# Block attention and MLP on one core: the same instructions in a new order, from a planner with other landing times and a charge for switches

## The chip, the cores and the metric

The kernel runs on one core of a Trainium2 chip. A core has TensorE (PE, matmuls and weight loads), VectorE (DVE), ScalarE (ACT), GpSimd (POOL), and SyncE (SP), which here issues the transfers. The metric is the device time of one execution in microseconds. The times before are 612.1, 612.23 and 613.61, median 612.23.

## The reference

An attention in which each query sees a band of 16 positions to either side and one summary for every block of 32 keys, and behind it an MLP with a gated activation.

```python
k_sum = k.reshape(B, H, nb, block, D).max(axis=3)          # B, H, S, D = 4, 8, 768, 64; block 32
v_sum = v.reshape(B, H, nb, block, D).mean(axis=3)
scores_l = where(|i - j| < 16, scale * q @ k^T, -1e9)
scores_s = scale * q @ k_sum^T + log(32)
a = softmax(concat([scores_l, scores_s]))
x = a @ concat([v, v_sum])                                 # 3072 tokens x 512
h = x @ w_in                                               # 512 x 2048
g = h * erf(maximum(h, 0) + log1p(exp(-|h|)))
out = g @ w_out                                            # 2048 x 512
```

## The kernel before

The 3072 tokens are worked on in 6 chunks of 512. For each chunk there are four blocks of attention (a pair of heads each) and four groups of the hidden layer (512 of the 2048 columns each). An attention block is: scores on PE (mask, window keys and key summaries; small matmuls of 64 rows), maximum on DVE, exponentials on ACT, normalisation on DVE or ACT, transposes of the weights, and the product with the values (16 small matmuls, tile px). The result is split in a rounded high part and a low rest (tiles xh, xl), and the MLP's products are three matmuls each on such parts: the hidden layer `h` (mm1, 128x512), in the later chunks sums of half-size products (`ha`, `hb`), and the output `ops` (mm2).

The order on every engine is found by a planner when the program is built. The code calls each step in a natural order and hands it to a class `Plan` with a cost in us for each engine that can do it, what it reads and what it writes. `Plan.order` then goes through time: it takes the engine that is free first, looks at the steps that are ready, and picks the one with the lowest key: its place in the natural order on PE, a due time on the other engines, each plus a correction from the table `TUNE`. A step that two engines can do goes to the one that ends first. Nothing of the plan's times is in the program; what stays is the order on each engine, and between engines the waits for data and for buffers. Engines work off their own order without overtaking.

Two things in it matter here. The first transfers are declared by `first_dma`, with a time in us that each occupies the transfer queue in the plan, in place of a size: keys and queries of the first block row (`load_qk_first`, tiles kf and qf), the values of the first sequence in two halves (`load_v_first`, vt), the window values (`load_vw_first`, vwf) and the first weights (rw). The value sums of the first sequence are six matmuls on the halves of the values (`vsum_first`, tile vs), three for each half. From them come the rows that are copied into the window values of each of the four blocks; for the last three blocks ACT or a transfer can do this copy. And where the plan sees PE idle before the first output product, the program puts filler matmuls (`busy`, tile idle), one for each 0.31 us of planned idle time:

```python
        if o["on"] == "PE":
            filling = filling and "o3" not in o["w"]
            if filling:
                busy(int(max(0.0, o["start"] - last) / 0.31))
            last = o["end"]
```

Of the kernel before, what the change touches and what calls it, by code (L numbers as in the profile page):

```python
# [23 lines left out]
NP = H // 2  # L24
# [6 lines left out]
LW = 96  # L31
# [5 lines left out]
MQ = NP  # L37
# [8 lines left out]
TABLE = 1.29  # L46
TTR = 1.52
# [9 lines left out]
class Plan:  # L57
# [6 lines left out]
    def add(self, eng, fn, r=(), w=(), after=(), table=None, hold=0.0, land=0.0):  # L64


        n, deps = len(self.ops), set(after)
        for x in r:
            deps.update(self.last.get(x, ()))
        for x in w:  # L70
            deps.update(self.last.get(x, ()))
            deps.update(self.readers.get(x, ()))
        for x in w:
            self.last[x], self.readers[x] = (n,), []
        for x in r:
            self.readers.setdefault(x, []).append(n)
        deps.discard(n)
        self.ops.append(dict(n=n, eng=eng, fn=fn, r=r, w=w, deps=deps, table=table, hold=hold, land=land))
        return n
# [22 lines left out]
    def order(self, free, window, tune, table):  # L102

        self.due()
        ops = self.ops
        wait = [len(o["deps"]) for o in ops]
        ready = [0.0] * len(ops)
        cand = {e: set() for e in free}  # L110
        pe = [o["n"] for o in ops if "PE" in o["eng"]]
        seq = {n: i for i, n in enumerate(pe)}
        head = 0
        done = [False] * len(ops)
        out = []
        key, change = {}, {}
        for o in ops:
            n = o["n"]
            later, change[n], which, eng = tune.get(n, (0.0, PEN, 0, None))
            key[n] = later + (n if "PE" in o["eng"] else o["due"])  # L120
            if eng is not None:
                o["eng"] = {eng: o["eng"][eng]}
                o["two"] = True
            if o["table"]:
                o["pick"] = o["table"][which]

        def open_(n):
            for e in ops[n]["eng"]:
                cand[e].add(n)

        for o in ops:
            o["two"] = o.get("two", False) or len(o["eng"]) > 1
            if not wait[o["n"]]:
                open_(o["n"])
        while len(out) < len(ops):
            best = None
            while head < len(pe) and done[pe[head]]:
                head += 1
            for e, c in cand.items():
                if e == "PE":  # L140
                    c = [n for n in c if seq[n] - head <= window(seq[n])]
                if not c:
                    continue
                t = max(free[e], min(ready[n] for n in c))
                if best is None or t < best[0]:
                    best = t, e, c
            t, e, c = best
            c = [n for n in c if ready[n] <= t + 0.05]
            n = min(c, key=lambda n: (key[n] + (change[n] if e == "ACT" and ops[n]["table"] and table not in ops[n]["table"] else 0.0), n))
            o = ops[n]  # L150
            if len(o["eng"]) > 1:
                ends = {x: max(free[x], ready[n]) + d for x, d in o["eng"].items()}
                x = min(ends, key=ends.get)
                if x != e and ends[x] < ends[e]:
                    cand[e].discard(n)
                    cand[x].add(n)
                    continue
            start = max(t, ready[n])
            end = start + o["eng"][e]
            if o["table"] and e == "ACT" and table not in o["table"]:  # L160
                table = o["load"] = o["pick"]
                end += TABLE
            free[e] = end
            o.update(on=e, start=start, end=end)
            done[n] = True
            out.append(o)
            if e == "SP":
                end += o["land"]
            for x in o["eng"]:
                cand[x].discard(n)  # L170
            for s in o["succ"]:
                ready[s] = max(ready[s], end + (LAT[e] if e == "SP" or e not in ops[s]["eng"] or ops[s]["two"] else 0.12 if e != "PE" else 0.0) + (ops[s]["hold"] if e != "SP" else 0.0))
                wait[s] -= 1
                if not wait[s]:
                    open_(s)
        return out
# [9 lines left out]
def block_attention_mlp(ctx: ExitStack, tc: tile.TileContext, q_t, k_nat, k_win, v_tok, v_nat, v_win, w_in, w_out, out):  # L186
# [78 lines left out]
    def pe(us, fn, r=(), w=(), **kw):  # L265
        return P.add({"PE": us}, lambda e: fn(), r, w, **kw)
# [10 lines left out]
    def first_dma(us, fn, r=(), w=(), **kw):  # L277
        return P.add({"SP": us}, lambda e: fn(), r, w, hold=2.0, land=-1.0, **kw)
# [210 lines left out]
    def load_qk_first(p):  # L489
        st[p] = dict(qb=qfs[:, p], vw=vws[p // 2][:, p % 2])  # L490
        first_dma(0.97, lambda: nc.sync.dma_start(out=kfirst[p], in_=k_nat[0, p]), w=[f"kf{p}"])
        first_dma(0.66, lambda: nc.sync.dma_start(out=qfs[:, p], in_=q_t[0, p]), w=[f"qf{p}"])

    def load_v_first():
        for n in range(2):
            first_dma(2.0, lambda n=n: nc.sync.dma_start(out=vts[n], in_=v_tok[3 * n:3 * n + 3].rearrange("t s c -> s t c")), w=[f"vt{n}"])

    def load_vw_first(p):
        first_dma(1.3, lambda: nc.sync.dma_start(out=st[p]["vw"], in_=v_win[0, p]), w=[f"vwf{p}"])
# [54 lines left out]
    def scores(qd, banks=PA):  # L554

        s = st[qd]

        def mask():
            for n in banks:
                tiles[n] = ps(n, n)  # L560
            s["sc"] = [tiles[n] for n in banks]
            m0 = mask_at[qd // NP % 3]
            for sc in s["sc"] if qd < MQ else []:

                nc.tensor.matmul(sc[:, 0:NI * NK], lhsT=ident_h, rhs=mask_h[:, m0:m0 + NI], start=True, stop=False, skip_group_check=True)
                nc.tensor.matmul(sc[:, 0:NI * NK].rearrange("q (i c) -> q i c", i=NI)[:, :, LW:NK], lhsT=ones, rhs=cst.rearrange("o (i c) -> o i c", i=NI), start=False, stop=False, skip_group_check=True)

        def keys(parts):
            for j in range(NB):
                for a in range(2):  # L570
                    r, o = slice(64 * a, 64 * a + 64), slice(64 * (j % 2), 64 * (j % 2) + 64)
                    for n, rhs in parts(r, j):
                        n += j // 2 * NK
                        nc.tensor.matmul(s["sc"][a][o, n:n + rhs.shape[-1]], lhsT=s["qb"][r, 64 * j:64 * j + 64], rhs=rhs, start=qd >= MQ, stop=True, skip_group_check=True)  # L574

        def near(r, j):

            kn, k0 = kfirst[qd], 64 * j - 16
            return [(0, kn[r, k0:k0 + LW])] if j else [(0, kn[r, 0:16]), (16, kn[r, 0:LW - 16])]

        def both():
            mask()
            keys(lambda r, j: [(0, s["kw"][r, j])])
        if qd >= NP:
            pe(1.06 if qd >= MQ else 1.64, both, [f"qb{qd % 2}", f"kw{qd % 2}"] + (["mh"] if qd < MQ else []), banks)
        else:
            pe(0.58, mask, ["mh"], banks)
            pe(0.96, lambda: keys(near), [f"qf{qd}", f"kf{qd}"], banks)
            pe(0.5, lambda: keys(lambda r, j: [(LW, ksum[r, 0, qd])]), [f"qf{qd}", f"ksum0{qd}"], banks)
# [47 lines left out]
    def transp(qd):  # L637
# [14 lines left out]
        if qd < DT:  # L652
            pe(0.95, go, [pr], PA)
            act(1.1, cp, PA, ["pt"])
            return
# [23 lines left out]
    def av(qd, bank):  # L679
        s = st[qd]  # L680
        s["bank"] = bank

        def go():
            xo = s["xo"] = ps("px", bank)
            for j in range(NB):
                o = slice(64 * j, 64 * j + 64)
                for a in range(2):
                    r = slice(64 * a, 64 * a + 64)
                    if qd < DT:
                        b = 64 * (NI * a + j // 2)  # L690
                        nc.tensor.matmul(xo[r, o], lhsT=s["vw"][0:NK, j, r], rhs=s["pt"][0:NK, j % 2, b:b + 64], start=True, stop=True)  # L691
                    else:
                        z = 2 * (j % 2)
                        nc.tensor.matmul(xo[r, o].rearrange("d (a q) -> d a q", a=2), lhsT=s["vw"][0:NK, j, r], rhs=s["pt"][0:NK, z:z + 2, NI * a + j // 2], start=True, stop=True)  # L694
        pe(1.08, go, ["pt", "vw"] if qd >= NP else ["pt", f"vwf{qd}", f"vwg{qd}"], [bank])
# [550 lines left out]
```

## Time and profile before

| what | us |
|---|---|
| median of 3 runs | 612.23 |
| the profiled execution's own time | 612.39 |
| its span, first to last instruction | 610.2 |
| PE busy with matmuls | 599.5 |
| DVE busy | 460.5 |
| ACT busy | 407.9 |

The mean granted TensorE clock is 0.996 of full speed. The page shows 40 slices of the span; PE is at 9 tenths or more in all but the first and the last. A row of a timeline has the start, the time, the engine, the line and operation, what is written and read, the shape, and in brackets idle time before it with its releaser. A releaser "issue" means that the engine waited for nothing that the profile shows. Matmuls overlap, so the distance between two starts is what one costs PE, and its own time is longer. SPq is SyncE's queue; a row there is the issue of a transfer, which lands later.

### The profile page before, as it was taken

The page shows a single profiled execution, that of the slowest core. Times are in us where ns is not written, and L with a number is a line of the kernel's source. Part 1 is how long each engine was busy: PE and PEld are TensorE (multiplying, and loading weights), DVE is VectorE, ACT ScalarE, POOL GpSimd, SP SyncE. Part 2 cuts the span into 40 slices and gives each one's busy share as a digit, 9 for nine tenths or more (in the row PEclk, how much of TensorE's full clock was granted, in tenths as well). Part 3 has the DMA queues.
Part 4 walks back from the last instruction along what each step waited for, and adds up shares of the span by engine and source line. Part 5 has one row for each costly group of instructions (what it writes and reads, how often), then busy time and mean ns, then how long its engine had stood idle before and what let it go on. Part 6 is the DMA issues. An engine that isn't in the chain of part 4 may idle for free.

```text
span 610.2 us, 12059 instructions
## 1 busy us (share of the span) xinstructions
PE 599.5 (98%) x4714; PEld 498.1 (82%) x4714; DVE 460.5 (75%) x915; ACT 407.9 (67%) x815; POOL 3.8 (1%) x28
## 2 busy tenths in 40 slices
PE   6999999999999999999999999999999999999997
PEld 4576656777888889889799899898898898899886
DVE  5899999969999997877889758669658537546442
ACT  5779959979789774873776764746667546652340
POOL 2000000000000000000000000000000000000000
PEclk9899999999999999999999999999999999999999
DMA  8979766568699689999898989888777774665622
GB/s 325 412 313 362 296 207 208 206 236 311 252 333 361 239 295 331 348 382 325 319 379 294 370 301 340 284 302 261 287 272 284 265 248 151 245 238 193 220 70 69
DMA packets 47751, 169.85 MB, mean 278 GB/s; under 512 B 4432, under 2 KB 17488, under 8 KB 35152
## 3 DMA queue, kind: packets, MB, share of 16 engines
q1 hardware_dynamic: 47120, 168.58, 76.2%
q8 instruction: 37, 0.61, 0.4%
q10 hardware_dynamic: 576, 0.52, 0.3%
q14 instruction: 18, 0.15, 0.1%
HBM read 135.66 MB, written 31.46 MB: 274 GB/s over the span
## 4 chain that ended last, share of the span: by engine, by line
PE 94%; ACT 2%; DVE 1%; DMA 1%; issue 1%; SPq 0%; ACTq 0%
PE ops L952 39%; PE hb L838 15%; PE h L797 14%; PE ha L838 11%; PE ops L948 5%; PE pA L574 3%; PE px L694 3%; PE vs L508 1%; DMA qf<-q_t 1%; PE px L691 1%; ACT prf L615 0%; ACT ptr L651 0%; PE pA L646 0%; ACT w L281 0%; PE pB L574 0%
## 5 line engine op out<-in xcount | busy, mean ns | idle before, releaser
L952 PE MATMUL ops<-w,gh 128*128 128x512 f32 x704 | 228.2, 393 | 0.0
L952 PEld LDWEIGHTS ops<-w,gh 128*128 128x128 f32 x704 | 132.6, 188 | 28.6 <-issue 1.1
L952 PE MATMUL ops<-w,gl 128*128 128x512 f32 x352 | 137.5, 391 | 0.0
L1203 ACT ACT_TABLE_LOAD x91 | 116.8, 1283 | 1.6
L928 DVE TENSOR_TENSOR hc<-wt,hc 128x1024 f32<-128x1024 f32 x44 | 52.8, 1221 | 60.7 <-ACT wt L916 60.6
L797 PE MATMUL h<-xh,w 128*128 128x512 f32 x256 | 86.8, 402 | 0.0
L281 ACT COPY hc<-hb 128x256 f32<-128x256 f32 x56 | 20.8, 371 | 85.5 <-DVE hc L891 31.3
L952 PEld LDWEIGHTS ops<-w,gl 128*128 128x128 f32 x352 | 66.2, 188 | 12.4
L615 ACT ACTIVATE prx<-prx,stats 128x120 f32<-128x120 f32 x160 | 61.0, 382 | 0.8 <-DVE stats L602 0.6
L797 PEld LDWEIGHTS h<-xh,w 128*128 128x128 f32 x256 | 48.0, 188 | 12.5 <-issue 1.1
L838 PE MATMUL hb<-w,ws 128*128 128x256 f32 x384 | 56.4, 283 | 0.0
L935 DVE TENSOR_TENSOR gl<-hc,gh 128x1024 fp32r<-128x1024 f32 x44 | 53.5, 1217 | 0.4
L838 PEld LDWEIGHTS hb<-w,ws 128*128 128x128 f32 x384 | 50.6, 192 | 0.1
L797 PE MATMUL h<-xl,w 128*128 128x512 f32 x128 | 50.2, 392 | 0.2 <-DVE xl L710 0.2
L916 ACT ACTIVATE wt<-wt 128x1024 f32<-128x1024 f32 x48 | 49.6, 1057 | 0.4
L904 ACT ACTIVATE wt<-hc 128x1024 f32<-128x1024 f32 x32 | 32.6, 1053 | 14.1 <-DVE hc L281 13.9
L281 DVE CAST gh<-hc 128x1024 fp32r<-128x1024 f32 x40 | 27.5, 688 | 11.2 <-PE ops L952 10.7
L659 DVE STREAM_TRANSPOSE ot<-prx 128x1024 f32<-128x1024 f32 x16 | 32.9, 2056 | 0.3
L615 ACT ACTIVATION_READ_ACCUMULATOR prx<-prx,stats 128x1 f32 x160 | 29.9, 187 | 0.0
L948 PE MATMUL ops<-a32s,gw 128*128 128x512 f32 x64 | 29.1, 597 | 0.0
L797 PEld LDWEIGHTS h<-xl,w 128*128 128x128 f32 x128 | 24.1, 188 | 6.0 <-DVE xl L710 1.0
L838 PE MATMUL ha<-xh,ws 128*128 128x256 f32 x128 | 28.3, 284 | 0.0
(166 smaller groups left out, 998.1 us busy)
## 6 DMA issues: line engine op xcount, KB each, us to landing
w<-dr SPq DMA_DIRECT2D x36, 1024.0 KB, 7.5
ws<-ds SPq DMA_DIRECT2D x30, 1024.0 KB, 6.5
vw<-v_win SPq DMA_DIRECT2D x20, 512.0 KB, 4.8
kw<-k_win SPq DMA_DIRECT2D x20, 480.0 KB, 3.5
rw<-w_in SPq DMA_DIRECT2D x8, 1024.0 KB
rw<-w_out SPq DMA_DIRECT2D x8, 1024.0 KB, 6.5
dr<-w SPq DMA_DIRECT2D x8, 1024.0 KB, 5.4
dt<-ot SPq DMA_DIRECT2D x16, 512.0 KB, 3.5
```

Source lines behind the costliest of these rows:

```text
L281: e.copy(o, i) if e is nc.scalar else e.tensor_copy(o, i)
L615: nc.scalar.activation(s["pr"][:, j], s["pr"][:, j] if qd >= MQ else s["sc"][j // NI][:, i * NK:(i + 1) * NK], AF.Exp, scale=-1.0 if qd >= ...
L659: e.transpose(out=s["ot"].rearrange("p k j q -> p j k q"), in_=prx.rearrange("p j (q k) -> p j k q", k=4))
L797: nc.tensor.matmul(hs[k, f][:, 0:T], lhsT=w[m], rhs=xt[ch, cc][x], start=(cc == 0 and n == 0), stop=(cc == 3 and n == 2))
L838: nc.tensor.matmul(shape, lhsT=w[m], rhs=y[l], start=first and c == 0 and i == 0, stop=c == 1 and i == 2, skip_group_check=True)
L904: nc.scalar.activation(wt[k, n], hc[k, n], AF.Softplus)
L916: act(0.96, lambda n=n: nc.scalar.activation(wt[k, n], wt[k, n], AF.Erf, scale=-1.0 if k < SOFT else 1.0), [s], [s], table=("sig",), after ...
L928: e.tensor_tensor(hc[k, n], wt.pop((k, n)), hc[k, n], op=ALU.mult)
L935: e.tensor_tensor(gs[k, n][1], hc.pop((k, n)), f32(gs[k, n][0]), op=ALU.subtract)
L948: nc.tensor.matmul(os_[ch, t], lhsT=x[0][:, i % 2, t * 128:(t + 1) * 128], rhs=w32["o", g, i // 2][:, i % 2], start=first, stop=last)
L952: nc.tensor.matmul(os_[ch, t], lhsT=x[y][:, i % 2, t * 128:(t + 1) * 128], rhs=w[m], start=first and n == 0, stop=last and n == 2)
L1203: nc.scalar.preload_act_table_set(sets[o["load"]])
```

## The change

The planner gets other numbers, and the order of every engine is made anew. The instructions are the same but for filler matmuls (11 behind the first seven before, 11 after, at other places) and for steps that now go to another of the engines that can do them: some hundred copies between DVE and ACT, and two of the row copies of the value sums from ACT to transfers.

- The second keys occupy the queue for 2.7 us in the plan, not 0.97; the two halves of the values 2.1 and 2.25, not 2.0; the window values 1.35, not 1.3.
- Steps of small matmuls are marked `small`. In the plan PE pays `SWITCH` = 0.09 us where such a step follows one of large matmuls.
- The costs of the small steps themselves are new: scores 0.98 and 1.56 (1.06 and 1.64), transposes 0.61 (0.95), products with the values 1.085 (1.08).
- The table `TUNE` is another one (1099 entries, before 1103).

```diff
 TABLE = 1.29
+SWITCH = 0.09
 TTR = 1.52
...
-    def add(self, eng, fn, r=(), w=(), after=(), table=None, hold=0.0, land=0.0):
+    def add(self, eng, fn, r=(), w=(), after=(), table=None, hold=0.0, land=0.0, small=False):
...
-        head = 0
+        head, was = 0, False
...
                 end += TABLE
+            if e == "PE":
+                end += SWITCH * (o["small"] and not was)
+                was = o["small"]
             free[e] = end
...
-        first_dma(0.97, lambda: nc.sync.dma_start(out=kfirst[p], in_=k_nat[0, p]), w=[f"kf{p}"])
+        first_dma(2.7 if p == 1 else 0.97, lambda: nc.sync.dma_start(out=kfirst[p], in_=k_nat[0, p]), w=[f"kf{p}"])
...
-            first_dma(2.0, lambda n=n: nc.sync.dma_start(out=vts[n], in_=v_tok[3 * n:3 * n + 3].rearrange("t s c -> s t c")), w=[f"vt{n}"])
+            first_dma(2.1 + 0.15 * n, lambda n=n: nc.sync.dma_start(out=vts[n], in_=v_tok[3 * n:3 * n + 3].rearrange("t s c -> s t c")), w=[f"vt{n}"])
...
-        first_dma(1.3, lambda: nc.sync.dma_start(out=st[p]["vw"], in_=v_win[0, p]), w=[f"vwf{p}"])
+        first_dma(1.35, lambda: nc.sync.dma_start(out=st[p]["vw"], in_=v_win[0, p]), w=[f"vwf{p}"])
...
-            pe(1.06 if qd >= MQ else 1.64, both, [f"qb{qd % 2}", f"kw{qd % 2}"] + (["mh"] if qd < MQ else []), banks)
+            pe(0.98 if qd >= MQ else 1.56, both, [f"qb{qd % 2}", f"kw{qd % 2}"] + (["mh"] if qd < MQ else []), banks, small=True)
...
-            pe(0.95, go, [pr], PA)
+            pe(0.61, go, [pr], PA, small=True)
...
-        pe(1.08, go, ["pt", "vw"] if qd >= NP else ["pt", f"vwf{qd}", f"vwg{qd}"], [bank])
+        pe(1.085, go, ["pt", "vw"] if qd >= NP else ["pt", f"vwf{qd}", f"vwg{qd}"], [bank], small=True)
```

What this does to the order is shown at three places. The first is SyncE's queue from its first transfer on; kf and qf are keys and queries of the four first blocks, vt the two halves of the values, rw a weight, vwf window values. Before:

```order
L491 DMA kf<-k_nat 128x768
L492 DMA qf<-q_t 128x512
L491 DMA kf<-k_nat 128x768
L492 DMA qf<-q_t 128x512
L491 DMA kf<-k_nat 128x768 x2
L492 DMA qf<-q_t 128x512
L496 DMA vt<-v_tok 128x3x512 x2
L317 DMA rw<-w_in 128x2048
L499 DMA vwf<-v_win 128x1024
L492 DMA qf<-q_t 128x512
L499 DMA vwf<-v_win 128x1024
L317 DMA rw<-w_in 128x2048
```

After:

```order
L495 DMA kf<-k_nat 128x768
L496 DMA qf<-q_t 128x512
L495 DMA kf<-k_nat 128x768
L496 DMA qf<-q_t 128x512
L500 DMA vt<-v_tok 128x3x512
L495 DMA kf<-k_nat 128x768
L496 DMA qf<-q_t 128x512
L500 DMA vt<-v_tok 128x3x512
L321 DMA rw<-w_in 128x2048
L495 DMA kf<-k_nat 128x768
L496 DMA qf<-q_t 128x512
L503 DMA vwf<-v_win 128x1024 x2
```

The first half of the values moved from eighth to fifth place, ahead of the third keys and queries; the fourth keys moved behind the second half and the first weight.

The second place is PE about the value sums (vs). Before, from the end of the third block's scores (banks o) into the fourth block's mask (bank h):

```order
L574 MATMUL o_238<-ksum,qf 64x24
L574 MATMUL o_239<-ksum,qf 64x24
L508 MATMUL vs<-vt,pick 120x512 x6
L565 LDWEIGHTS small
L565 MATMUL h_322<-mask_h,small 128x480
L566 LDWEIGHTS small
L566 MATMUL h_322<-small 128x4x24
```

After, from the end of the second block's scores (banks h) into the third block's (banks o), whose masks now stand ahead of the second block's scores:

```order
L578 MATMUL h_182<-ksum,qf 64x24
L578 MATMUL h_183<-ksum,qf 64x24
L993 LDWEIGHTS zeros
L993 MATMUL idle<-zeros 128x512
L512 MATMUL vs<-vt,pick 120x512 x2
L578 MATMUL o_191<-kf,qf 64x16
L578 MATMUL o_191<-kf,qf 64x80
L578 MATMUL o_192<-kf,qf 64x16
L578 MATMUL o_192<-kf,qf 64x80
```

Two of the six sum matmuls moved ahead of the third block's scores, with a filler before them; two more stand behind these scores, and the last two behind the fourth block's mask. Where two calls share a row, x2 counts both.

The third place is PE later on, at a product with the values (px) in the second chunk. Before, it stands alone among large matmuls:

```order
L952 MATMUL ops<-w,gl 128x512
L952 MATMUL ops<-w,gh 128x512
L694 MATMUL px<-ptd,vw 64x64 x16
L952 MATMUL ops<-w,gh 128x512
L952 MATMUL ops<-w,gl 128x512
```

After, a product with the values is followed at once by scores (pA, pB):

```order
L801 MATMUL h<-xl,w 128x512
L801 MATMUL h<-xh,w 128x512
L698 MATMUL px<-ptd,vw 64x64 x16
L578 MATMUL pA<-kw,qb 64x120
L578 MATMUL pB<-kw,qb 64x120
```

There PE goes from large to small matmuls once for two steps. Counted over the order behind the first 16 products of the hidden layer, visits to small matmuls (scores, transposes, products with the values) went from 35 to 30.

On DVE the maximum of the first block's scores moved ahead of the second key summary; on ACT the two copies of the first transposed weights moved ahead of the copy of the value sums.

## Rows read from the trace of the kernel before

**Rows 1.** The page's busy times: us, share of the span, instructions.

```profile
PE 599.5 (98%) x4714; PEld 498.1 (82%) x4714; DVE 460.5 (75%) x915; ACT 407.9 (67%) x815; POOL 3.8 (1%) x28
```

**Rows 2.** Who waited for whom on PE: us in total, times, longest.

```profile
PE o L574 <- issue: 2.2, 1, 2.2
```

**Rows 3.** Stretches: length; busy us (instructions) of PE, PEld, DVE, ACT, POOL; PEclk, DMA.

```profile
15.44:18.86 3.42, 3.42 (x6) 1.31 (x5) 3.32 (x6) 2.81 (x16) 0.00 (x0) 0.50 1.04 411
45.00:100.00 55.00, 55.00 (x339) 34.48 (x339) 54.86 (x106) 46.88 (x81) 0.00 (x0) 1.00 0.74 262
```

**Rows 4.** Timeline of PE to 48 us.

```profile
6.47 0.38 PE L565 MATMUL h<-mask_h,small 128*128 128x480 bf16 x1
...
7.94 0.97 PE L574 MATMUL h<-kf,qf 64*64 64x16 f32 x36 [0.80 <-DMA qf<-q_t]
...
9.28 0.38 PE L565 MATMUL o<-mask_h,small 128*128 128x480 bf16 x1
...
14.34 7.11 PE L508 MATMUL vs<-vt,pick 128*120 128x512 f32 x12
21.29 0.37 PE L565 MATMUL h<-mask_h,small 128*128 128x480 bf16 x1
...
25.26 0.27 PE L646 MATMUL pA<-ident,prf 64*120 64x64 f32 x1
...
25.88 1.47 PE L989 MATMUL idle<-zeros 128*128 128x512 bf16 x6
27.04 0.54 PE L797 MATMUL h<-xh,w 128*128 128x512 f32 x1
...
47.98 0.27 PE L466 MATMUL vt<-ident,vs_sum 128*120 128x128 f32 x1
```

**Rows 5.** Transfer queue: two issues of its timeline, and one of its waits.

```profile
10.45 0.33 SPq L499 DMA_DIRECT2D vwf<-v_win  x1
12.47 2.61 SPq L317 DMA_DIRECT2D rw<-w_in  x2
...
SPq L317 <- DMA vt<-v_tok: 3.6, 2, 1.9
```

**Rows 6.** Timelines of DVE and ACT in the first 24 us.

```profile
7.18 0.95 DVE L502 TENSOR_REDUCE ksum<-kf 128x24 f32<-128x768 f32 x1 [2.54 <-DMA kf<-k_nat]
8.05 0.65 DVE L608 TENSOR_REDUCE stats<-pA 128x4 f32<-128x480 f32 x1
...
9.57 0.36 ACT L615 ACTIVATE prf<-pA,stats 128x120 f32<-128x120 f32 x1 [5.13 <-DVE stats L609]
...
12.27 0.40 ACT L615 ACTIVATE prf<-h,stats 128x120 f32<-128x120 f32 x1
...
21.49 0.58 ACT L512 COPY vsum<-vs 24x512 f32<-24x512 f32 x1 [3.23 <-PE vs L508]
22.10 1.04 ACT L281 COPY vwf<-vsum 24x1024 f32<-24x1024 f32 x1
23.17 0.58 ACT L651 COPY ptr<-pA 120x512 f32<-120x512 f32 x1
```

**Rows 7.** Timeline of PE about one product with the values.

```profile
174.81 0.39 PE L952 MATMUL ops<-w,gl 128*128 128x512 f32 x1
175.04 0.39 PE L952 MATMUL ops<-w,gh 128*128 128x512 f32 x1
175.36 1.15 PE L694 MATMUL px<-ptd,vw 120*64 120x64 f32 x32
176.44 0.50 PE L952 MATMUL ops<-w,gh 128*128 128x512 f32 x1
176.78 0.39 PE L952 MATMUL ops<-w,gl 128*128 128x512 f32 x1
```

**Rows 8.** The page's instruction queue (packets, MB), and one kind of transfer (us to landing).

```profile
q8 instruction: 37, 0.61, 0.4%
...
vw<-v_win SPq DMA_DIRECT2D x20, 512.0 KB, 4.8
```

More of the change, by code (lines that the diff above doesn't have):

```diff
@@ L77, in add @@
         deps.discard(n)
-        self.ops.append(dict(n=n, eng=eng, fn=fn, r=r, w=w, deps=deps, table=table, hold=hold, land=land))
+        self.ops.append(dict(n=n, eng=eng, fn=fn, r=r, w=w, deps=deps, table=table, hold=hold, land=land, small=small))
         return n
@@ L584, in scores @@
         if qd >= NP:
-            pe(1.06 if qd >= MQ else 1.64, both, [f"qb{qd % 2}", f"kw{qd % 2}"] + (["mh"] if qd < MQ else []), banks)
+            pe(0.98 if qd >= MQ else 1.56, both, [f"qb{qd % 2}", f"kw{qd % 2}"] + (["mh"] if qd < MQ else []), banks, small=True)
         else:
-            pe(0.58, mask, ["mh"], banks)
-            pe(0.96, lambda: keys(near), [f"qf{qd}", f"kf{qd}"], banks)
-            pe(0.5, lambda: keys(lambda r, j: [(LW, ksum[r, 0, qd])]), [f"qf{qd}", f"ksum0{qd}"], banks)
+            pe(0.58, mask, ["mh"], banks, small=True)
+            pe(0.96, lambda: keys(near), [f"qf{qd}", f"kf{qd}"], banks, small=True)
+            pe(0.5, lambda: keys(lambda r, j: [(LW, ksum[r, 0, qd])]), [f"qf{qd}", f"ksum0{qd}"], banks, small=True)
     def softmax(qd, banks=PA):
```

2 lines of the change are left out of this document (1 added, 1 removed).

## The prediction

> **What bounds the kernel now.** I read the page's busy times first: TensorE (PE) is busy for 599.5 of the 610.2 us span [rows 1]. So only what makes PE wait, or makes it slower while it is busy, can be worth anything. Next I read who waited for whom on PE. One entry stands out: 2.2 us before a score matmul, which ended by "issue", so the profile shows nothing that PE waited for [rows 2]. It lies at 11.98 to 14.18 us. Then the stretches: from 45 us on PE is busy all the time (55.00 of 55 us), and VectorE (DVE) nearly so (54.86). Right behind the 2.2 us wait there is a stretch of 3.42 us at a granted clock of 0.50, the lower of the two levels, 1.2 GHz [rows 3]. So there are two places to look at: the first 47 us, where PE waits, idles with filler matmuls and runs slowly, and the price of alternation in the long part behind it.
>
> How much do the first 47 us lose? From 27.04, where the first hidden-layer product starts, to 47.98 PE does 18 such products, of which 2 belong to the next group [rows 4]. One takes three matmuls of 0.23 [rows 7], 0.68 us; so the first 16 end at 47.98 - 2 x 0.68 = 46.6. These 19.6 us hold 16 x 0.68 + 3 attention products of 1.08 [rows 7] + 2 rounds of transposes of 0.62 (25.26 to 25.88 [rows 4]) = 15.4 us of work. 4.2 us are lost there to waits, fillers and alternation. Before 27.04 there are the 2.2 us, 1.16 us of filler (25.88 to 27.04) and the slow stretch, which costs half of 3.42, 1.7 us.
>
> **The change, part by part.** *Order of the first transfers.* The third pair of keys and queries, and the fourth keys, stood ahead of the first half of the values (vt). Now that half is fifth. The last query of the old order landed at 10.45 and the half of the values at 12.47: these issues wait for those landings (the queue reuses a small set of semaphores, and "DMA vt" is the releaser of the second) [rows 5]. So the half takes 2.0 us. Behind the query that lets PE start at 7.94 [rows 4] it now lands at about 7.8 + 2.0 = 9.8. The third keys and queries follow it. Old, 1024 KB landed between 7.8 and 10.45, 0.39 KB per ns; their 640 KB take 1.65 us, until 11.5.
>
> *VectorE.* The old order put the second key summary ahead of the first maximum: DVE stood until 7.18 for the keys, and the maximum began at 8.05 [rows 6], though the scores were there at 6.47, where the next mask starts [rows 4]. Swapped, the maximum runs from 6.6 to 7.9 (two of 0.65), the summary ends at 7.9 + 0.87 = 8.8, and the first exponentials start at 8.1, not 9.57 [rows 6].
>
> *PE until the wait.* The second scores start at 7.94 as before, since their transfers are unmoved; the third mask, now ahead of them, fills 0.5 us of that wait. They take 1.34 (7.94 to 9.28) and end near 9.6, as their last part waits for the later summary. Then come two sum products of the values. Six took 6.95 us (14.34 to 21.29 [rows 4]); less the 1.7 of the slow clock that is 0.87 each. From 9.8 on they end at 11.6. The third scores follow, whose queries are there, until 13.0 (11.6 + 1.34).
>
> *The 2.2 us wait.* No row says what it is; it sat just before the last matmul of the third scores. I bound it: gone, the scores end at 13.0; of its old length, at 15.2. I take an end at the old moment, 14.2, thus 1.1 us of wait. Why: the new order puts only some ten instructions more ahead of that matmul, and PE starts the second scores at 7.94 in both. One queue carries instructions, 37 packets in all [rows 8]; against 4714 matmuls and as many weight loads [rows 1] that is one packet per 255 PE instructions. A load of code, begun at a certain instruction near 8 us, would end when it did.
>
> The Trainium skill ("Runtime: NRT & Kernel Launch", Instruction fetch mechanics) says that an engine's program comes in blocks of 256 instructions, loaded ahead, and that crossing a block costs something "mostly hidden". The size agrees with the 255 above. By that rule the 2.2 us wouldn't be code, it would have no reason to come again, and the gain would be larger by the 1.1 us (first rival). I keep 1.1, because no transfer of data and no engine ends that wait.
>
> *From 14.2 on.* Maximum 1.3, to 15.6. ScalarE (ACT) does the third exponentials in 2.7 (9.57 to 12.27), to 18.4; the sum copy takes 0.61 (21.49 to 22.10), and the two copies of transposed weights, as wide, 1.1 before it; a row copy 1.07 (22.10 to 23.17) follows, to 21.2 [rows 6]. PE meanwhile has four sum products, a mask, the fourth scores and two rounds of transposes, 4 x 0.87 + 0.5 + 1.34 + 2 x 0.62 and some alternation, 7 us, to 21.2, so the first attention product runs from 21.4 to 22.5. ACT goes on with a weight copy and a row copy of 1.07 each and the next two copies, to 24.4, then the split, as wide as a copy, 0.6, to 25.0, and DVE's half of it to 25.7. PE's third transposes wait for the copies (24.6 to 25.2), the second attention product for the split (25.9 to 27.0). At 27.0 PE is then where it was at 27.04, with one attention product and one round of transposes more behind it: 1.7 us. The sum products done in the old waits, and the clock that isn't lost, are inside this figure and not added again; most of them pays only for ACT, which bounds this part.
>
> Still to do are 16 products, 2 attention products and 1 round of transposes, 13.7 us. Four or five alternations at 0.1 a side cost 0.5. Two row copies now go from ACT to transfers; ACT still normalises the fourth block late, near 32.8, so transposes wait for it some 0.5 us; I add 0.4 for others. End: 27.0 + 13.7 + 0.5 + 0.9 = 42.1. Old: 46.6. **Gain 4.5 us.**
>
> *Alternation.* The last matmul before a small one takes 175.04 to 175.36, and the first one behind it 176.44 to 176.78, where a plain one takes 0.23 (174.81 to 175.04) [rows 7]. One visit to small matmuls costs 0.32 + 0.34 - 2 x 0.23 = 0.20 us. By the order, in the part behind the first 16 products PE pays 35 such visits before and 30 now, the small matmuls being the same. **Gain 5 x 0.20 = 1.0 us**, since PE is never idle there.
>
> *The rest.* Some hundred copies move between DVE and ACT, and transfers of weights move on the queue. I cost these at nothing: what hides them is that PE has other products ready, as its 55.00 of 55 us shows. Without that cover each us of DVE would be a us of PE (third rival).
>
> Sum: 5.5 us. The profiled execution took 612.39 us, 2.2 more than its span, which I leave. 612.39 - 5.5 = 606.9. The median of the runs is 0.16 below the profiled one, so **606.8 us**.
>
> **Rivals.**
> *The 2.2 us wait doesn't come again.* Then the third scores end at 13.0, and all that hangs on ACT comes 1.1 earlier: 605.7. For it: nothing in the trace names its cause, and a cause in the old order of transfers would go with it. Against it: the place in the instruction stream is the same.
>
> *The wait in full, or the slow clock again.* PE is still to wait 0.2, 2.1 and 0.7 us between 21 and 26. Filler matmuls stand in the order there, as they did from 25.88, behind which no lower clock shows. If they don't hold it, the same half-speed stretch costs 1.7 us; the wait in full costs 1.0. Time 607.8 to 609.5. The Trainium skill ("TensorE: Matmul & The Clock Gate", Part 1: The HAM clock gate) says that the low level is the default and activity releases it; the trace agrees in so far as 0.50 stands right behind PE's longest wait [rows 2, 3], and the rule speaks for the fillers.
>
> *DVE sets the pace.* It is busy 54.86 of 55 us [rows 3]. If it isn't only filled there but bounds, PE's lead is worth what DVE can follow. The lead at 27.0 was 1.7, and what comes behind it may all be given back: 1.7 + 1.0 = 2.7, thus 609.5, and up to 610.3 if DVE follows less. Against it: PE had no wait for DVE in 45 to 100.
>
> *The row copies hold the transfer queue (slower).* The two row copies from ACT now are transfers, and the queue issues in order. The first can't be issued before the sums are there and its window values have landed, near 24.4; the values of the fourth pair, which were issued at 10.45 [rows 5], and a weight load stand behind it. If the transfers run dry at both copies, each costs about one issue to landing, 4.8 us for a load of window values [rows 8], so 9.6 in all. PE would come out 9.6 - 5.5 = 4.1 us slower, 616. It decides from 5.5 us of delay on. Against it: when the first copy is released a 1 MB weight load should still be moving, 2.5 us.
>
> *The new order does less than it says:* the waits reappear under other names, and the time stays within 1.8 us of the old one.
>
> **How the numbers follow.** Forecast 0.50 (605.9 to 608.4: the wait as taken, and each other term 0.5 us to either side), the wait gone 0.17 (604.4 to 606.2), wait in full or clock 0.10, DVE 0.11, no change 0.06, slower by the queue 0.06. The range reaches from 604.4 to 610.3, the end of the DVE rival; outside are the last two cases and some beyond the low end. A measurement of this kernel can tell about 0.3%, 1.8 us, from no change, so faster means under 610.4: 0.50 + 0.17 + 0.10 + 0.11, less 0.03 for the edge of the DVE case, 0.85. Same 0.09, slower 0.06.
>
> **What would show it.** The first sum products should start near 9.8, the third scores end near 14.2 with about 1 us of idle, no stretch of 0.50 should follow, and the first exponentials should start near 8.1. The first hidden-layer product should still stand near 27, and the 16th end near 42. From there to the end PE should gain about 1 us more, and the span be near 604.7. I am wrong if the values land near 12.5 in spite of the order, if the 16th product ends behind 45, or if PE shows new waits for DVE or weights between 45 and 120.

## The result, and the profile after

The changed kernel takes 606.89 us (605.98 to 607.62, 4 runs), the kernel before beside it 612.16 (610.83 to 613.61, 4 runs): a ratio of 0.9913 with an interval of 0.9886 to 0.9939. It is 5.3 us faster; forecast were 5.4, a time of 606.8. The profiled execution took 607.62, its span is 605.8, 4.4 less than before. A second set of runs of the same kernel gave 606.50 (6 runs) and a profile with a span of 604.3, so two profiled executions of one kernel can lie 1.5 us apart.

The page's busy times, to be set against [rows 1]:

```profile
PE 597.3 (99%) x4714; PEld 498.3 (82%) x4714; DVE 459.6 (76%) x907; ACT 412.1 (68%) x823; POOL 3.8 (1%) x28
```

Who waited on PE, against [rows 2] (us in total, times, longest):

```profile
PE hb L842 <- DVE stats L606: 1.0, 1, 1.0
PE o L578 <- issue: 0.9, 1, 0.9
PE h L578 <- DMA qf<-q_t: 0.6, 1, 0.6
PE px L698 <- DMA ptd<-dt: 0.3, 1, 0.3
PE vs L512 <- DMA vt<-v_tok: 0.3, 1, 0.3
```

The "issue" wait is back, with 0.9 us in place of 2.2. The wait for `stats` is in both kernels (1.0 us, late in the program).

The stretches that answer to [rows 3], and the one in which the copies of the value sums go through the queue:

```profile
15.40:18.80 3.40, 3.40 (x26) 1.64 (x25) 3.26 (x8) 2.28 (x14) 0.00 (x0) 1.00 1.07 416
30.00:47.00 17.00, 17.00 (x143) 13.75 (x142) 16.90 (x21) 14.17 (x25) 0.00 (x0) 1.00 0.94 366
45.00:100.00 55.00, 54.94 (x346) 33.31 (x345) 54.90 (x107) 45.12 (x93) 0.00 (x0) 1.00 0.83 290
```

No stretch of 0.50 follows the wait, and PE is without a gap from 30 to 100 us, apart from 0.06 us.

PE's timeline, against [rows 4]:

```profile
8.55 0.97 PE L578 MATMUL h<-kf,qf 64*64 64x16 f32 x36 [0.62 <-DMA qf<-q_t]
...
10.55 1.95 PE L512 MATMUL vs<-vt,pick 128*120 128x512 f32 x4 [0.27 <-DMA vt<-v_tok]
12.42 0.97 PE L578 MATMUL o<-kf,qf 64*64 64x16 f32 x36
13.16 0.60 PE L578 MATMUL o<-ksum,qf 64*64 64x24 f32 x25
14.64 0.31 PE L578 MATMUL o<-ksum,qf 64*64 64x24 f32 x7 [0.89 <-issue]
14.88 1.98 PE L512 MATMUL vs<-vt,pick 128*120 128x512 f32 x4
...
22.75 1.15 PE L695 MATMUL px<-ptr,vwf 120*64 120x64 f32 x32
...
28.43 0.50 PE L801 MATMUL h<-xh,w 128*128 128x512 f32 x1
...
44.28 0.27 PE L470 MATMUL vt<-ident,vs_sum 128*120 128x128 f32 x1
```

The first two sums run at 10.55, ahead of the third scores (12.42); four sum matmuls (two sums) take 1.9 us, while in [rows 4] twelve took 7.11 with the slow clock. The last row is the first transpose of the summaries, 18 hidden-layer products behind the start as in [rows 4]: 44.28 against 47.98. I use it below as **the mark**: at it the new order leads by 3.7 us, and behind it gains 4.4 - 3.7 = 0.7 more by the spans.

The second profile of the same kernel has the same order 1.0 to 1.2 us earlier, since its second queries landed earlier (scores at 7.59):

```profile
9.54 1.95 PE L512 MATMUL vs<-vt,pick 128*120 128x512 f32 x4 [0.15 <-DMA vt<-v_tok]
...
27.21 0.50 PE L801 MATMUL h<-xh,w 128*128 128x512 f32 x1
...
43.06 0.27 PE L470 MATMUL vt<-ident,vs_sum 128*120 128x128 f32 x1
```

By it the lead at the mark is 4.9 us, and 1.0 more comes behind it.

ACT, DVE and the queue, against [rows 5, 6]:

```profile
8.43 0.36 ACT L619 ACTIVATE prf<-pA,stats 128x120 f32<-128x120 f32 x1 [3.99 <-DVE stats L613]
...
16.52 0.36 ACT L619 ACTIVATE prf<-o,stats 128x120 f32<-128x120 f32 x1 [2.14 <-DVE stats L623]
```

```profile
47.62 1.22 DVE L927 TENSOR_TENSOR gw<-wt,hc 128x1024 f32<-128x1024 f32 x1
```

```profile
24.98 0.99 SPq L520 DMA_DIRECT2D vwf<-vsum  x1
...
30.30 0.83 SPq L520 DMA_DIRECT2D vwf<-vsum  x1
```

The first exponentials start at 8.43, not 9.57. The gate's multiply (gw), which feeds the first output products, will be needed below. The two rows of the queue are the row copies that ACT no longer does.

### The profile page after: what moved, and what is told of

Same layout as the page of the kernel before. It is cut to its first block, busy times and chain, and to the rows that moved or that the text cites. A ratio compares the mean times of both kernels' runs of the same rounds, so it can differ in the third digit from the quotient of the medians.

```text
span 605.8 us, 12063 instructions
## 1 busy us (share of the span) xinstructions
PE 597.3 (99%) x4714; PEld 498.3 (82%) x4714; DVE 459.6 (76%) x907; ACT 412.1 (68%) x823; POOL 3.8 (1%) x28
## 4 chain that ended last, share of the span: by engine, by line
PE 85%; DVE 8%; DMA 3%; issue 1%; ACT 1%; SPq 0%; ACTq 0%
PE ops L956 38%; PE hb L842 14%; PE ha L842 11%; PE h L801 11%; PE px L698 3%; PE pA L578 3%; PE ops L952 2%; DMA ptd<-dt 1%; DMA vt<-v_tok 1%; DVE a L344 1%; PE vs L512 1%; DVE w L363 1%; DVE a L347 1%; PE px L695 1%; DVE ot L663 1%
## 5 line engine op out<-in xcount | busy, mean ns | idle before, releaser
L285 ACT COPY hc<-hb 128x256 f32<-128x256 f32 x66 | 24.5, 372 | 93.5 <-PE hb L842 41.6
```

The lines of the kernel that those rows point to most:

```text
L285: e.copy(o, i) if e is nc.scalar else e.tensor_copy(o, i)
```

## The experiments

In the experiments' kernels the planner's search is replaced by its result, a list of steps in the order in which they are issued; the steps' code is the same, and its lines stand 59 (in the kernels with other first fillers 62 at the fillers) below those of the changed kernel. FILL says how many filler matmuls stand ahead of which step:

```diff
-    plan = P.order(free, ...)
+    for x in SEQ.split():
+        o = ops[int(x[:-1])]
+        o["on"] = {"P": "PE", "D": "DVE", "A": "ACT", "S": "SP", "G": "POOL"}[x[-1]]
+        plan.append(o)
```

All were timed in five rounds against the kernel before on the same chip, whose median was 612.0 to 612.4.

**The start alone, and the rest alone.** Two lists joined of both orders, split near 42 us: in the first kernel the start is the changed one, in the second the rest.

```diff
-SEQ = changed order
+SEQ = changed order of all that its plan starts before 41.9, then the order of before
```

> Every engine's order of the changed kernel up to the 18th product of the hidden layer (44.3 us in its trace), and of the kernel before from there on. Theory: the gain is made at the start. There PE is ahead by 46.62 - 42.92 = 3.7 us, and the old order behind it has no use for the lead but to keep it: 612.2 - 3.7 = 608.5. Rival A, DVE sets the pace from 45 to 120 us: the old order, whose copies lie more on DVE, gives the lead back, 610 to 612. Rival B, the gain lies in the order of the long part: about 611.5.

> The other half: every engine's order of the kernel before up to the 18th product of the hidden layer, and of the changed kernel from there on. Theory: only the five visits to small matmuls fewer are gained, 5 x 0.20 = 1.0 us, less what the trace of the changed kernel shows of new waits (0.4): 611.3 to 611.6. Rival B, the gain lies in the long part: 607 to 608.5. In the trace PE should start the summary transposes behind the 18th product at 48.0, as before, and end about 1 us earlier than before.

The start alone: 614.19, ratio 1.0034 (1.0017 to 1.0052), slower than before, and outside what the theory (608.5) and its rivals (610 to 612) had. PE's waits, its mark and the output products, DVE's multiply, and a stretch:

```profile
PE ops L1011 <- DVE gw L986: 3.3, 1, 3.3
...
PE pA L637 <- ACT kw L344: 0.9, 1, 0.9
```

```profile
42.77 0.27 PE L529 MATMUL vt<-ident,vs_sum 128*120 128x128 f32 x1
...
53.06 6.23 PE L1011 MATMUL ops<-a32s,gw 128*128 128x512 f32 x10 [3.31 <-DVE gw L986]
```

```profile
51.70 1.22 DVE L986 TENSOR_TENSOR gw<-wt,hc 128x1024 f32<-128x1024 f32 x1
```

```profile
53.95:57.37 3.42, 3.42 (x5) 1.35 (x4) 3.38 (x5) 3.38 (x6) 0.00 (x0) 0.50 1.02 318
```

PE passes the mark at 42.77, 5.2 ahead of before, and then stands for 3.3 us for gw. DVE comes to gw at 51.70, where it did in the kernel before, for its order has weight conversions, a summary and a maximum ahead of it:

```profile
51.92 1.22 DVE L923 TENSOR_TENSOR gw<-wt,hc 128x1024 f32<-128x1024 f32 x1
```

Behind that wait the clock falls to 0.50, which costs another half of 3.42. So the 5.2 us of lead met 3.3 + 0.9 of waits and 1.7 of slow clock, 5.9 in all (6.4 by the spans): given back, with interest.

The rest alone: 610.69, ratio 0.9976 (0.9959 to 0.9993), with the issue wait of 2.3 us and this stretch behind it:

```profile
13.82:17.24 3.42, 3.19 (x5) 1.54 (x6) 2.68 (x8) 2.64 (x16) 0.00 (x0) 0.50 1.00 405
```

1.35 us by the medians, 0.8 by the spans; between the theory (611.3 to 611.6) and its rival (607 to 608.5). The two parts don't add: -2.15 and +1.35 alone, 5.3 together.

**The start and the next group.** To see whether the lead is kept if DVE's order goes with it, the split was moved to 90 us.

```diff
-SEQ = changed order of all that its plan starts before 41.9, then the order of before
+SEQ = changed order of all that its plan starts before 90, then the order of before
```

> The changed kernel's order for everything that its plan starts before 90 us (over a group of the hidden layer longer than in the earlier hybrid, which switched at 42 us and lost its whole lead), the order of before from there on. Theory: the lead of the start (3.7 us at the end of the first 16 hidden-layer products) is kept only if the order of the next group goes with it, above all VectorE's gate multiply (gw) ahead of the maximum, and TensorE's next hidden-layer products ahead of the first output products. Then no wait of 3 us for gw appears, and the time is 612.1 - 3.7 = 608.4 (607.6 to 609.2). Rival: the lead is given back wherever the old order begins, since VectorE sets the pace in it: 611 to 614, with a wait of over 1 us of the products for gw or of pA/pB for ACT somewhere behind 90 us.

608.2, ratio 0.9932 (0.9919 to 0.9944). The mark:

```profile
43.60 0.27 PE L529 MATMUL vt<-ident,vs_sum 128*120 128x128 f32 x1
```

The theory's number was 608.4, and the rival, that the lead goes wherever the old order begins, is out: it begins at 90 here. PE shows no wait for gw. With the changed order between 42 and 90 us, DVE does gw at 46.92, ahead of the maximum, and PE has the next group's hidden-layer products ahead of the output products:

```profile
46.92 1.22 DVE L986 TENSOR_TENSOR gw<-wt,hc 128x1024 f32<-128x1024 f32 x1
```

```profile
53.81 10.46 PE L1011 MATMUL ops<-a32s,gw 128*128 128x512 f32 x24
```

That is 6 us less than with the split at 42. Which of the two moves keeps the lead isn't shown: with DVE's old order gw would have ended near 51.70 + 1.22 = 52.9, still in time for output products at 53.81.

**The issue wait.** PE's first seven filler matmuls of 512 columns became 28 of 128, as long in sum. PE thereby comes earlier to any given number of instructions; nothing else changes.

```diff
-    busy(WARM)
+    for _ in range(28):
+        nc.tensor.matmul(idle[:, 0:128], lhsT=zeros[:, 0:128], rhs=zeros[:, 0:128], start=True, stop=True)
```

> The changed kernel with its first 7 filler matmuls of 512 columns replaced by 28 of 128 columns, about the same PE time but 42 more PE instructions ahead of the first scores. Theory of the wait by issue: it is a load of program code that starts when PE reaches a certain instruction (in both traces it ends 6.0 to 6.1 us behind PE's 194th instruction) and blocks PE at a later one. 42 instructions more bring the start forward from the second to the first block's scores, by about 2 us, so the load ends near 12.8, when PE is just at the place: the 0.9 us of wait go, or shrink to under 0.2, and all behind comes 0.9 earlier: 606.0. Rival: the wait belongs to the third scores themselves (their data, their bank): 0.9 us of wait before their last matmul as now, 606.9.

> The kernel before with the same 28 fillers of 128 columns for its first 7. If the wait by issue is a load of code, it ends near 12.3 and not at 14.18; the value sums start when their data is there, near 12.5; the clock doesn't fall behind it, so the six sums end near 17.8 and not at 21.29. ACT, which stood 3.2 us for these sums, goes on at once, and the first hidden-layer product comes about 3 us earlier: 609.2. Rival: the wait isn't code: 2.2 us and the stretch of 0.50 stay, 612.2. If the first holds, most of what the new order gains could have been had without it.

The changed kernel so: 606.13, ratio 0.9905 (0.9882 to 0.9928). The kernel before so: 609.78, ratio 0.9971 (0.9955 to 0.9987). The third scores of the first, and the mark:

```profile
12.93 0.67 PE L637 MATMUL o<-ksum,qf 64*64 64x24 f32 x32
13.52 1.98 PE L571 MATMUL vs<-vt,pick 128*120 128x512 f32 x4
...
43.00 0.27 PE L529 MATMUL vt<-ident,vs_sum 128*120 128x128 f32 x1
```

The key summaries' 32 matmuls run through, where the changed kernel has 25, a wait of 0.89 and 7 more. In the second the wait is 0.4 and the clock holds:

```profile
PE o L637 <- issue: 0.4, 1, 0.4
```

```profile
13.00:17.00 4.00, 3.99 (x10) 1.78 (x11) 3.80 (x9) 4.00 (x26) 0.00 (x0) 1.00 1.03 413
```

So that wait goes by PE's instructions, as a load of code does. The traces' records of single instructions and packets show it more closely. In all seven profiles with this wait PE stands before its 444th to 446th matmul or weight load, and goes on 2.3 to 2.6 us after a packet of 16,384 bytes begins on the instruction queue (at 11.57 in the kernel before, 12.21 in the changed one, 9.65 in the second kernel here). In the other seven PE comes to that instruction 2.4 us or more after the packet begins, and doesn't wait; the start alone, above, is one of them (packet at 10.56). With the slow clock behind it the wait was worth 612.04 - 609.78 = 2.3 us of the old time. The new order is still 3.65 us better when both have these fillers.

**What the first places in the order are worth.** One move of the start was undone in each of three kernels.

```diff
 L1052 MATMUL idle<-zeros 128x512
-L571 MATMUL vs<-vt,pick 120x512 x2
 L637 MATMUL o_191<-kf,qf 64x16
...
-L571 MATMUL vs<-vt,pick 120x512 x2
+L571 MATMUL vs<-vt,pick 120x512 x4
```

> The changed kernel with one move undone on TensorE: the first two sums of the values stand behind the third block's scores, not ahead. Theory: the issue wait inside the third scores ends at a moment that a load of code sets, not at a number of matmuls behind it. So the third scores end near 14.8 us as now, the wait grows from 0.9 to about 2, and the two sums (1.7 us) come on top behind it; part of that is hidden, since ScalarE bounds the stretch behind: 607.6 to 608.6, with a longer issue wait (1.7 to 2.5 us). Rival 1: the third scores end earlier by the two sums, the rest follows, nothing is lost: 606.5 to 607.2, issue wait at most 1 us. Rival 2: the whole 1.7 us shows and the half-speed clock comes back behind the longer wait: 609.5 to 610.5.

610.6, ratio 0.9956 (0.994 to 0.9972): 3.7 us lost, and not as the theory had it. There is no issue wait. The third scores wait for their queries, which now land behind the values, and the clock falls:

```profile
11.95 1.72 PE L637 MATMUL o<-kf,qf 64*64 64x16 f32 x36 [2.33 <-DMA qf<-q_t]
...
14.38 5.42 PE L571 MATMUL vs<-vt,pick 128*120 128x512 f32 x8
```

```profile
11.95:14.38 2.43, 2.43 (x69) 2.38 (x69) 1.61 (x4) 1.76 (x11) 0.00 (x0) 0.50 1.03 422
14.38:17.00 2.62, 2.62 (x5) 1.11 (x4) 2.40 (x6) 0.98 (x6) 0.00 (x0) 0.50 1.01 396
17.00:19.80 2.80, 2.80 (x8) 0.94 (x8) 2.77 (x4) 1.87 (x12) 0.00 (x0) 0.84 1.05 418
```

The second kernel has the first ten transfers in the old order and every engine's order as changed:

```diff
 L555 DMA qf<-q_t 128x512
-L559 DMA vt<-v_tok 128x3x512
-L554 DMA kf<-k_nat 128x768
-L555 DMA qf<-q_t 128x512
-L559 DMA vt<-v_tok 128x3x512
-L380 DMA rw<-w_in 128x2048
-L554 DMA kf<-k_nat 128x768
+L554 DMA kf<-k_nat 128x768 x2
+L555 DMA qf<-q_t 128x512
+L559 DMA vt<-v_tok 128x3x512 x2
+L380 DMA rw<-w_in 128x2048
```

> The changed kernel with the first ten transfers in the order of before (third and fourth keys and queries ahead of the values); every engine's own order as in the changed kernel. Theory: the first half of the values lands near 12.5 us, not 10.4; the first two sums and the third scores behind them shift by 2.1, but 0.9 of that was idle time anyway: third scores end near 16.0 against 14.8, time 607.8 to 608.6. Rival 1: ScalarE bounds what follows, nothing is lost: 606.5 to 607.2. Rival 2: all of the landing's delay shows and the clock falls in the longer wait: 609 to 611.

609.76, ratio 0.9952 (0.994 to 0.9964): 2.9 us lost, again more than the theory gave, and again with a slow stretch behind a wait for data:

```profile
12.59 2.75 PE L571 MATMUL vs<-vt,pick 128*120 128x512 f32 x4 [1.92 <-DMA vt<-v_tok]
15.28 1.71 PE L637 MATMUL o<-kf,qf 64*64 64x16 f32 x36
```

```profile
12.59:15.28 2.69, 2.69 (x5) 0.69 (x5) 1.53 (x4) 2.18 (x14) 0.00 (x0) 0.69 1.03 413
15.28:17.42 2.14, 2.14 (x70) 2.11 (x69) 0.00 (x0) 0.00 (x0) 0.00 (x0) 0.59 1.03 405
```

The third has DVE's second key summary ahead of the first maximum, as before:

```diff
-L565 TENSOR_REDUCE ksum<-kf 128x24
+L565 TENSOR_REDUCE ksum<-kf 128x24 x2
 L671 TENSOR_REDUCE stats<-pA 128x4
...
-L565 TENSOR_REDUCE ksum<-kf 128x24
```

> The changed kernel with one move undone on VectorE: the second key summary stands ahead of the first block's maximum, as before. Theory: the first exponentials start 1.4 us later (near 9.6), but ScalarE then has to wait for the third maximum, behind the scores that the issue wait holds, in either case; so nothing is lost: 606.4 to 607.3. Rival: ScalarE bounds the start from its first exponentials on and all of the 1.4 us shows: 608.0 to 608.6.

606.71, ratio 0.9901 (0.9887 to 0.9916): nothing lost. ACT's first exponentials start later and the third at about the same time:

```profile
9.34 0.36 ACT L678 ACTIVATE prf<-pA,stats 128x120 f32<-128x120 f32 x1 [4.89 <-DVE stats L672]
...
16.09 0.36 ACT L678 ACTIVATE prf<-o,stats 128x120 f32<-128x120 f32 x1 [1.15 <-DVE stats L682]
```

**Clock or displacement.** The waits of the two kernels that lost were filled with 8 and 7 filler matmuls; nothing else was changed. The edit of the first (in the second, step 42 gets 8 in place of 1):

```diff
-FILL = {73: 1, 85: 6, 78: 3, 36: 1}
+FILL = {73: 1, 85: 6, 78: 3, 36: 9}
```

> The kernel with the sums behind the third scores, which took 610.6 us (3.7 more than the changed kernel) with a wait of 2.33 us for the third queries and then a granted clock of 0.50 from 11.95 to 17.0 and 0.84 to 19.8. Added: 8 filler matmuls of 128x512 in that wait. Theory: the loss is mostly clock. At half speed 2.43 + 2.62 us lost half, 2.5 us, and the rest 0.16 x 2.8 = 0.45, 3.0 in all. The fillers end the fall; left is the displacement of the two sums, 0.7 to 1.7 us: 607.6 to 608.7, no stretch of 0.50, summary transposes on TensorE near 44.5 to 46, not 47.23. Rival 1: the loss is displacement, what hangs on ScalarE comes as late with a full clock: 609.8 to 610.8, and the transposes stay near 47. Rival 2: the fillers don't hold the clock: 610 to 611, with the 0.50 stretch.

> The kernel with the old order of the first transfers, which took 609.76 us (2.9 more than the changed kernel) with a wait of 1.92 us for the first half of the values and then a granted clock of 0.69 over 2.69 us and 0.59 over 2.14 us. Added: 7 filler matmuls of 128x512 in that wait. Theory: the clock cost 0.31 x 2.69 + 0.41 x 2.14 = 1.7 us, and 1.2 is the later landing: 608.0 (607.5 to 608.6), no slow stretch, summary transposes near 45.2, not 46.86. Rival 1: the landing costs all of it, since ScalarE bounds what follows: 609.4 to 610.2, transposes near 46.8. Rival 2: the fillers don't hold the clock: the same time, with the slow stretch.

608.59, ratio 0.9948 (0.993 to 0.9966), and 608.46, ratio 0.9947 (0.9928 to 0.9967). Full clock in the same stretch of the profiled executions, first and second:

```profile
11.95:17.00 5.05, 5.05 (x79) 2.74 (x76) 4.88 (x11) 4.20 (x25) 0.00 (x0) 1.00 1.03 408
```

```profile
11.95:17.00 5.05, 4.77 (x77) 2.60 (x76) 3.33 (x8) 2.65 (x16) 0.00 (x0) 1.00 1.03 410
```

Their marks stand at 44.91 (47.23 without the fillers) and 44.98 (46.86). So of the 3.7 us that the sums' old place costs 2.0 were clock, and of the 2.9 of the old transfers 1.3; 1.7 and 1.6 are the later work itself.

The other executions agree, and show that the fall of the clock doesn't come every time. With the sums in their old place, four of six executions had a mean granted clock of 0.994 (610.6 to 611.2 us) and two 1.000 (608.1 and 608.8). With the fillers it was 0.997 in four of twelve (610.2 to 610.9) and 1.000 in eight (607.9 to 608.8). With the old transfers it was 0.996 or 0.997 in all five, with the fillers there 0.996 in one of twelve. So the fillers change how often the clock falls, and hardly the time at full clock. The kernel before, over all its executions beside these experiments, had 0.999 or 1.000 in 12 of 74 (median 610.2) and less in 62 (median 612.4).

**Once more, side by side.** The changed kernel and the one with 28 small fillers, on one chip in the same rounds; the edit is the one above.

> The changed kernel once more, beside the next one on the same chip and in the same rounds: 606.5 to 607.3 by every theory.

> The changed kernel with its first seven filler matmuls of 512 columns replaced by 28 of 128 columns, once more, to be set against the changed kernel run beside it. Theory: PE comes earlier to the instruction that starts the code load, the issue wait of 0.9 us is gone, and 0.6 to 1.3 us of it arrives at the end: 605.6 to 606.4, 0.5 to 1.2 us under the changed kernel. Rival: the earlier median of 606.13 was chance, and the two agree within 0.4 us.

606.50 (606.04 to 607.32, 6 runs) and 605.99 (605.29 to 606.26, 6 runs), ratios to before of 0.9903 (0.9874 to 0.9933) and 0.989 (0.9864 to 0.9917). The version with small fillers is the faster in both sets, by 0.5 to 0.8 us; the intervals overlap, so this small step is likely and not settled.

## Why the prediction was right, step by step

**The first transfers and the sums: right.** Predicted were sum products from 9.8; they ran at 10.55, since the queries ahead of them landed late in this execution (scores at 8.55 against 7.94), and the wait for the values was 0.3. In the second profile they ran at 9.54. The second half of the reason was missing: the prediction counted the sums as work done earlier. The runs show that they also stand in the gap until the third queries land, which these transfers moved behind the values. Without them PE idles 2.33 us there, and the clock falls.

**DVE's swap: right in time, of no value.** The exponentials came at 8.43 (predicted 8.1), but undoing it costs nothing: the third exponentials wait for the third maximum, and so for PE, in either order. The prediction didn't add it as a term of its own.

**The issue wait: right.** Predicted 1.1 us, ending near 14.2; it was 0.9, ending at 14.64, and 0.7, ending at 13.43, in the second profile. That it is a load of code was an argument from a count of packets that no row assigns to PE; the kernels with 28 small fillers bear it out, since they change PE's instruction count alone and the wait goes (0.9 to none, 2.2 to 0.4). So does the place of the wait: the same instruction in seven profiles, shortly behind such a packet. The Trainium skill ("Runtime: NRT & Kernel Launch", Instruction fetch mechanics) has such crossings as "mostly hidden"; here one was not, and the measurement decides.

**No slow clock: right.** Granted 1.00 behind the 0.89 us wait, and a mean of 0.999 or 1.000 in all ten executions of the changed kernel (median 606.7). Against the 610.2 of the kernel before at such a clock that is 3.5 us; the other 1.8 of the 5.3 go with the slow clock.

**ACT's chain: 1.4 us too early by the first profile, right by the second.** The first hidden-layer product came at 28.43, not 27.0. The third exponentials started at 16.52, not 15.6: the scores ended 0.7 later than forecast, and the releaser in the row is a step of the normalisation (L623) that DVE does behind the maximum. The first attention product followed at 22.75, not 21.4. In the second profile these two products stand at 27.21 and 21.53. So the lateness is this execution's, from its queries on, and not the chain's.

**From there to the 16th product: 0.6 us too slow.** I gave 15.1 us, 0.9 of it for waits on the fourth block. No such wait came; by the mark the 16th product ended at 44.28 - 2 x 0.68 = 42.9, 14.5 behind 28.43, and it was the same 14.5 in the second profile. The gain was 46.6 - 42.9 = 3.7, not 4.5. The second profile has the mark at 43.06, a gain of 4.9; 4.5 lies between the two.

**Alternation: the size holds, the cause isn't shown alone.** Predicted 1.0 behind the 16th product; by the spans it was 0.7 here and 5.9 - 4.9 = 1.0 in the second profile, and the changed rest by itself gave 0.5 behind the mark by its profile (its mark stands at 47.67, 0.3 ahead) and 1.35 by the medians. Fewer visits to small matmuls fit that, but no run changed the visits and nothing else.

**The rest at nothing: right in number, and the reason holds only for the new order.** I wrote that the moved copies are hidden because PE has other products ready, and read that off the old order's 55.00 of 55 us. The start with the old order behind it shows that there PE had not: once it came earlier, it stood for DVE 3.3 us. The rival that DVE sets the pace is true of the old order, and worse than I priced it (614.2, not 609.5 to 610.3). It didn't come true because the new table also remade the order behind the start, with gw ahead of the maximum and more products of PE's ahead of the output. The prediction didn't look at either, so that the sum came out is in this part luck. Had I set DVE's time of gw (51.92) against a PE that comes 4.5 us earlier, I would have seen that the gain hangs on that order.

**The sum.** 4.5 and 1.0 were forecast; the two profiles give 3.7 and 0.7, and 4.9 and 1.0. The last step of the forecast rounds up: 612.39 - 5.5 - 0.16 is 606.7.

**The row copies on the queue: no price.** They were issued at 24.98 and 30.30, and PE was busy for 17.00 of 17.00 us from 30 to 47 and waited behind 24.98 only 0.4 us, for ACT's copies.

## What to carry to other kernels

A lead won at the start of a program can be lost whole behind it (5.2 us here), where another engine is just as busy, and kept if the order there is made anew too: look for the first step there for which the leading engine will wait, and at what stands ahead of it. An idle TensorE can pay twice, once for the wait and once for the clock behind it, so a gap that can't be closed is worth filling (1.3 and 2.0 us here). And a wait that ends for no reason in the profile may be a load of code: see whether it comes at the same count of instructions; more, shorter instructions ahead of it moved it here at no cost.

## What the runs showed of the hardware

In the profiled executions, waits of PE of 1.9 us (for values), 2.2 to 2.3 (for queries, and without a releaser) and 3.3 (for DVE) were each followed by a stretch at 0.50 or a mean of 0.59 to 0.69, whatever had ended the wait; those of 0.9, 0.7 and 0.6 us by none, and neither was the one of 1.7 below. Filling the wait kept the clock at 1.00 there, and made the fall rarer over all executions, which was worth 1.3 and 2.0 us by the medians. How long a wait must be isn't settled by this: the same kernel had the fall in some executions and not in others.

The wait for the transposed weights that come through memory (px, released by the transfer of `ptd`) is not steady: near 268 us it was 0.3 in the changed kernel, none in its second profile, and 1.7 with DVE's swap undone, where nothing near it in the order differs. The last one:

```profile
268.43 1.15 PE L757 MATMUL px<-ptd,vw 120*64 120x64 f32 x32 [1.69 <-DMA ptd<-dt]
```

That profiled execution took 608.57 us, the other three of its kernel 606.6 to 606.7. The 1.5 us between the two profiles of the changed kernel have another source for the most part: 1.2 of them are there at the mark, and the wait is 0.3.
